# Seven block products instead of eight for six more token tiles, with their operand forms made inside the first MLP pass

## Chip, cores, metric

The kernel runs on one core of a Trainium2 chip. The metric is device time in microseconds (us), the median over runs. TensorE (PE) does the matmuls, with its weight loads shown apart (PEld); VectorE (DVE), ScalarE (ACT) and GpSimd (POOL) do everything elementwise; SyncE (SP) issues nearly all DMAs. PE writes to PSUM (banks 0 to 7 in the kernel), and in the trace each engine runs its instructions in the order in which the program emitted them.

## What is computed

One transformer block on 2048 tokens of width 640, all float32:

```python
xn  = layernorm(x)
qkv = xn @ wqkv                                   # 32 heads of 20
phi = concat(softmax(p), softmax(-p)),  p = q or k @ w_phi   (per head)
o   = phi_q (phi_k^T v) / (phi_q (phi_k^T 1) + 1e-6)          # linear attention
out = x + o @ wo + gelu(layernorm(xn) @ w1 + b1) @ w2 + b2    # 1728 hidden units
```

Each float32 operand is split into a high and a low part, and a product is three matmuls (high·high, high·low, low·high).

## The kernel before, in words

**Layout.** Tokens are cut into four blocks of 512 (b = 0 to 3), each of four tiles of 128 (t = 0 to 15); the 640 features are five slices of 128 (c = 0 to 4). `y[b]` holds the normalised input of block b as a high and a low part.

**Stage 1, first MLP pass (to 212 us).** `Mlp.passes(g, b, ws)` handles two hidden groups of 128 (pass g = 0 to 6) for block b = 0 or 1. Its first half computes the two hidden groups, five three-matmul products each; `gelu` then puts GELU and the rounding to the high part on ACT and the low part on DVE. Its second half, emitted after the first half of the next pass, computes five output columns of two products each into PSUM banks 5, 6 and 7 in turn (`self.po`), and DVE adds each column to `acc[b]` (L338). So the fourth column can't start before DVE has read the first one, and the fifth not before the second. After each second half `take` splits a weight tile: two roundings on ACT (L60), two differences on POOL (L63).

`tick()` is called after every three-matmul product (0.68 us of PE), and advances a generator, `mlp.beside`, that emits other work between the products. In this stage it is `prep()`, whose list `events` holds a tick for each step: it loads slices of x for blocks 2 and 3 (`xs[c, b]`, tile name `xq`), centres them (POOL, L797), scales them (DVE, L800), rounds them (ACT, L804), takes the low part and stores both parts to DRAM (DVE L808 and SP L810). For each pair of slices q = 0, 1 it then combines them in place for the later MLP pass (`combine`, POOL L820). For q = 0 the list starts at `base` = 8, for q = 1 at 52. A tick fixes only the order in which steps join the queues; when they run depends on what they wait for.

For blocks 0 and 1 `turned_forms()` makes differences of the four 128 by 128 blocks of y ("forms"), their high and low parts, and stores them in `f_dram`.

**Stage 2, projections (212 to 426 us).** For each token tile q, k and v are computed against weights held in `wkv_`. An ordinary tile (`plan_part`) takes two parts of 512 columns, one of 320, and one of 512 for v: 15 matmuls each. Tiles 2 to 7 go in pairs instead (`plan_pair`): the two 512-column parts of two tiles and two row slices form 2x2 block products, which take seven products of sums of blocks instead of eight (names a11, s1 to s4 for weights, b11, t1 to t4 for the input); the fifth row slice is added plainly (`rest`). `load_forms(t)` fetches the forms of a pair from `f_dram` into tile `w0`. `plan_sums` makes s1 to s4. The feature maps follow as chains of steps on DVE, POOL and ACT (`plan_features`), and `plan_kv` accumulates phi_k^T v two tiles later. `plan_wo` splits a fifth of the output weights: load, round, subtract, store.

A planner (`Plan`) orders all this: each step has an engine, a cost and the steps it follows, due times are counted back from PE's order, and it emits the queues accordingly. The last eight parts (`TAIL`) belong to tiles 14 and 15.

**Stage 3** is the MLP for blocks 2 and 3 with the attention's second half beside it, then the output product.

Of the kernel before, what the change touches and what calls it, by code (L numbers as in the profile page):

```python
# [8 lines left out]
F32 = mybir.dt.float32  # L9
# [6 lines left out]
P = 128  # L16
# [34 lines left out]
def tile_kernel(ctx: ExitStack, tc: tile.TileContext, x, xT, wkT, wqT, wv, wphi, wo, w1, b1, w2, b2,  # L51
# [43 lines left out]
    f_dram = [tc.dram_tile([2, P, 2, 2, 2, 2 * P], F32, name=f"f{b}") for b in range(2)]  # L95
# [670 lines left out]
    def prep():  # L766
        ahead = []
        more = more_stats()
        for i, job in enumerate(jobs):
            for k, _ in enumerate(prep_fold(job, ahead, None if i else first_done)):  # L770
                if k == 0 and i < 6:
                    ahead = raws(jobs[i + 1])
                if i > 0 and k % 3 == 1:
                    next(more, None)
                yield

        for _ in more:
# [12 lines left out]

        def load(c, b):
            xs[c, b] = gp.tile([P, 512], F32, name="xq", bufs=4)
            with tc.issue_after(loads[1]):
                nc.sync.dma_start(xs[c, b], xT[c * P:(c + 1) * P, b * 512:(b + 1) * 512])

        def centred(c, b):
            nc.gpsimd.tensor_tensor(xs[c, b], xs[c, b], mr[b][:, 0], op=ALU.subtract)  # L797

        def scaled(c, b):
            nc.vector.tensor_tensor(xs[c, b], xs[c, b], mr[b][:, 1], op=ALU.mult)  # L800

        def hi(*at):
            hls[at] = gp.tile([P, 2, 512], F32R, name="t")
            nc.scalar.activation(hls[at][:, 0], xs[at], AF.Copy)  # L804

        def lo(*at):
            hl = hls.pop(at)
            nc.vector.tensor_tensor(hl[:, 1], xs[at], f(hl[:, 0]), op=ALU.subtract)  # L808
# [12 lines left out]

        def combined_lo(q, i):
            at = combined(q, i)[0]
            hl = hls.pop(at)
            nc.vector.tensor_tensor(hl[:, 1], xs[at], f(hl[:, 0]), op=ALU.subtract)
            nc.sync.dma_start(t_dram[q][:, i], f(hl))

        for n, step in enumerate(raw_sums(0, temps)):
            events.append((118 + 3 * n, len(events), step, ()))
        base = 8  # L830
        for q in range(3):
            tiles = [(c, b) for c in range(2 * q, min(2 * q + 2, KC)) for b in range(2, 4)]
            for n, at in enumerate(tiles):
                late = 6 * (at == (KC - 1, 3))
                for after, step in ((-6, load), (0, centred), (3, scaled), (5 + late, hi), (7 + late, lo)):
                    events.append((base + 5 * n + after, len(events), step, at))
            base += 5 * len(tiles) + 5
            if q < 2:
                for n, i in enumerate((0, 2, 1, 3)):
                    for after, step in ((0, combine), (3, lambda q, i: hi(*combined(q, i)[0])), (5, combined_lo)):  # L840
                        events.append((base + 4 * n + after, len(events), step, (q, i)))
                base += 19
        tick = 0
        for at, _, step, args in sorted(events, key=lambda e: e[:2]):
            while tick < at:
                tick += 1
                yield
            step(*args)
# [281 lines left out]
            nc.sync.dma_start(ed[q], ets[b][n][32 * q:32 * q + 32])  # L1130

    fts, ets = {}, {}
    SPLITS = [(8, 1), (8, 3), (9, 1), (9, 3), (10, 1)]
# [5 lines left out]
    def load_y(b):  # L1139

        y[b] = [yp.tile([P, KC, 512], F32R, name=f"y{p}{b % 2}") for p in range(2)]
        for p in range(2):
            nc.sync.dma_start(f(y[b][p]), y_dram[b - 2][p])

    def load_forms(t):
# [196 lines left out]
        if (t, 1 - n) in got:  # L1342
            plan_features(t, "k", j, got[t, 0][0], got[t, 1][0])

    at, got = {}, {}
    yts = {}

    def plan_pair(t):
# [41 lines left out]
        def bank_of(i):  # L1390
            return lambda: held[i]

        z = pe(a, "a11", "b11", True)
# [7 lines left out]
        z = pe(a, "s3", "t3", False, *z12)  # L1401
# [15 lines left out]
        _, q = plan_narrow(t, 0, a)  # L1417
        plan_features(t, "q", 2, d21[1], q)
        plan_wide(t, b1)
        plan_kv(t - 1, c)  # L1420
        _, q = plan_narrow(t + 1, 1, a)
        plan_features(t + 1, "q", 3, d22[1], q)
        plan_wide(t + 1, b1)

    def next_forms(t):
        if t < 6:
            yts[t + 2] = load_forms(t + 2)
        else:
            for q in range(2):
                for p in range(2):  # L1430
                    nc.sync.dma_start(f(wkv_[p][:, 2 * q, 512:1024]), s_dram[:, q, p])

    def plan_sums():

        last = [rp.tile([P, D], F32R, name=f"r{1 + p}")[:, :512] for p in range(2)]
        ways = [mtile(5, F32R), mtile(6, F32R)]
        ways = [third(0), *([w[:, p] for p in range(2)] for w in ways), last]
        ts = wp.tile([P, 4, D], F32, name="w0").rearrange("p i d -> p (i d)")
        ts = [ts[:, i * 512:i * 512 + 512] for i in range(4)]

        def splits(q, ts, ways, after):
            ops = []
# [31 lines left out]
        acc[2] = own["a"].tile([P, KC, 512], F32, name="acc2")  # L1474
        load_acc(2)

    def plan_wo(kc, *after):

        raw = {}

        def load():
            raw["lo"] = rp.tile([P, D], F32, name="r1")
            nc.sync.dma_start(raw["lo"], wo[kc * P:(kc + 1) * P, :])

        def hi():
            raw["hi"] = rp.tile([P, D], F32R, name="r2")
            nc.scalar.activation(raw["hi"], raw["lo"], AF.Copy)

        def lo():
            nc.gpsimd.tensor_tensor(raw["lo"].bitcast(F32R), raw["lo"], f(raw["hi"]), op=ALU.subtract)  # L1490

        def store():
            for w, wd in zip((f(raw["hi"]), raw["lo"]), wo_dram):
                nc.sync.dma_start(wd[:, kc, :], w)

        a = plan.add("SP", 0.7, load, *after)
        b = plan.add("ACT", 0.66, hi, a)
        c = plan.add("POOL", 1.9, lo, b)
        return [plan.add("SP", 1.4, store, c)]

    def first_weights():
        nonlocal mlp
# [35 lines left out]
        plan_part(t, i, n % 3)  # L1538
    for op in thirds:
        op[3] = (*op[3], at[1, 1])  # L1540
    for t in range(2, 8, 2):
        if t == 4:
            plan.add("PE", 0.0, lambda: load_y(2))
        plan_pair(t)
    plan.add("PE", 0.0, lambda: load_y(3))
    n, wo_done = 0, ()
    for t, i in [(t, i) for t in range(8, 14) for i in range(4)] + TAIL:
        plan_part(t, i, n % 3)
        n += 1
        tk = {(15, 1): 13, (15, 3): 14}[t, i] if (t, i) in ((15, 1), (15, 3)) else t - 2 if t < 15 and i == max(1, 10 - t) else None  # L1550
        if tk is not None:
            plan_kv(tk, n % 3)
            n += 1
        if (t, i) == (9, 0):
            plan.add("SP", 3.0, load_acc2, at[t, i])
        if (t, i) in SPLITS:
            wo_done = plan_wo(SPLITS.index((t, i)), at[t, i], *wo_done)
# [621 lines left out]
```

## Time and profile before

| | |
|---|---|
| median of 3 runs | 699.6 us (699.12 to 699.75) |
| the profiled execution | 699.7 us, its span 697.9 us |
| PE busy | 690.7 us (99%) |
| PEld, DVE, POOL, ACT busy | 582.0, 538.3, 493.7, 373.0 us |
| DMA | 117.06 MB, mean 168 GB/s |
| granted TensorE clock | 1.000 |

The span runs from the first to the last instruction. Successive matmuls overlap, so the rows show each at 0.39 us although a 512-column one starts about every 0.227 us. In a timeline row the columns are start, duration (of all merged instructions, with their count as x), engine, line, operation, output and inputs; a bracket gives idle time before it and what ended it.

### The profile page before, as it was taken

How to read it: one execution, taken by the hardware profiler on the slowest of the kernel's cores; microseconds unless marked ns; L12 is line 12 of the kernel's file. 1: busy time of each engine (PE TensorE's matmuls, PEld its weight loads, DVE VectorE, ACT ScalarE, POOL GpSimd, SP SyncE). 2: the span in 40 equal slices, each digit the busy share in tenths (PEclk: the TensorE clock that was granted, in tenths of full speed). 3: DMA queues.
4: the chain of work that ended last, by engine and by line, in shares of the span. 5: the costliest groups of instructions: out<-in, count | busy, mean ns of one | idle time of the engine just before them, and what ended most of it. 6: DMA issues, size and time to landing. Idle time of an engine off the chain costs nothing.

```text
span 697.9 us, 9867 instructions
## 1 busy us (share of the span) xinstructions
PE 690.7 (99%) x3313; PEld 582.0 (83%) x3313; DVE 538.3 (77%) x889; ACT 373.0 (53%) x633; POOL 493.7 (71%) x368
## 2 busy tenths in 40 slices
PE   9999999999999999999999999999999999999998
PEld 7888888888888888888888888888888888888886
DVE  7769564888766989997879778948678687689783
ACT  6435654444443644545554636457676666659350
POOL 3717684756267587889899879648689997677930
PEclk9999999999999999999999999999999999999999
DMA  9816857674622115554723736774355648871222
GB/s 328 261 50 192 245 160 230 222 250 161 203 93 124 61 62 210 137 170 170 170 76 99 178 101 256 225 215 128 110 159 159 180 152 295 283 277 60 77 75 106
DMA packets 72376, 117.06 MB, mean 168 GB/s; under 512 B 8054, under 2 KB 36502, under 8 KB 70318
## 3 DMA queue, kind: packets, MB, share of 16 engines
q1 hardware_dynamic: 69846, 114.32, 51.2%
q10 hardware_dynamic: 2480, 2.11, 1.0%
q8 instruction: 26, 0.43, 0.3%
q14 instruction: 24, 0.20, 0.1%
HBM read 76.62 MB, written 39.79 MB: 167 GB/s over the span
## 4 chain that ended last, share of the span: by engine, by line
PE 95%; DVE 3%; issue 1%; DMA 0%; ACT 0%; DVEq 0%; ACTq 0%
PE bank L996 23%; PE bank L69 19%; PE bank L70 19%; PE bank L71 19%; PE bank L1367 4%; PE bank L1109 2%; PE bank L650 2%; PE bank L1720 1%; PE bank L1721 1%; PE bank L1371 1%; PE bank L556 1%; PE bank L314 1%; PE bank L334 1%; PE bank L315 1%; PE bank L333 1%
## 5 line engine op out<-in xcount | busy, mean ns | idle before, releaser
L69 PE MATMUL bank<-m,w 128*128 128x512 f32 x288 | 112.9, 392 | 0.0
L70 PE MATMUL bank<-m,w 128*128 128x512 f32 x288 | 112.2, 390 | 0.5 <-DVE m L63 0.5
L71 PE MATMUL bank<-m,w 128*128 128x512 f32 x266 | 103.6, 389 | 0.0
L996 PE MATMUL bank<-wkh,y 128*128 128x512 f32 (+1 forms) x360 | 101.0, 355 | 0.0
L69 PE MATMUL bank<-y,w 128*128 128x512 f32 (+1 forms) x256 | 99.6, 389 | 0.4 <-DVE v L1095 0.4
L70 PE MATMUL bank<-y,w 128*128 128x512 f32 (+1 forms) x256 | 98.8, 386 | 0.0
L71 PE MATMUL bank<-y,w 128*128 128x512 f32 (+1 forms) x246 | 95.0, 386 | 0.0
L63 POOL TENSOR_TENSOR w<-r,w 128x640 fp32r<-128x640 f32 x29 | 49.5, 1719 | 34.6 <-ACT w L60 28.1
L996 PEld LDWEIGHTS bank<-wkh,y 128*128 128x128 f32 x360 | 65.0, 188 | 8.1
L70 PEld LDWEIGHTS bank<-m,w 128*128 128x128 f32 x288 | 54.1, 188 | 11.8 <-DVE m L63 0.9
L996 PE MATMUL bank<-wkl,y 128*128 128x512 f32 (+1 forms) x180 | 63.6, 354 | 0.0
L69 PEld LDWEIGHTS bank<-m,w 128*128 128x128 f32 x288 | 54.1, 188 | 11.4 <-issue 0.4
L71 PEld LDWEIGHTS bank<-m,w 128*128 128x128 f32 x266 | 49.9, 188 | 10.4
L338 DVE TENSOR_TENSOR acc<-bank,acc 128x512 f32<-128x512 f32 x70 | 47.2, 683 | 13.6 <-PE bank L71 8.0
L996 PE MATMUL bank<-w,y 128*128 128x512 f32 x240 | 57.5, 391 | 0.0
L69 PEld LDWEIGHTS bank<-y,w 128*128 128x128 f32 x256 | 48.1, 188 | 10.9 <-DVE v L1095 0.5
L1036 DVE TENSOR_REDUCE sm<-m 128x64 f32<-128x1280 f32 x32 | 47.1, 1471 | 11.8 <-ACT m L1031 11.8
L70 PEld LDWEIGHTS bank<-y,w 128*128 128x128 f32 x256 | 48.1, 188 | 9.4
L1028 POOL TENSOR_TENSOR m<-m,mx 128x640 f32<-128x640 f32 x32 | 45.9, 1434 | 12.2 <-DVE w L1061 5.7
L71 PEld LDWEIGHTS bank<-y,w 128*128 128x128 f32 x246 | 46.2, 188 | 9.4
L1031 ACT ACTIVATE m<-m,rs_all 128x1280 f32<-128x1280 f32 x32 | 43.7, 1366 | 16.4 <-POOL m L1028 16.4
L1714 POOL TENSOR_TENSOR e<-e,m 128x512 fp32r<-128x512 f32 x28 | 41.7, 1491 | 15.1 <-ACT m L1713 15.0
(291 smaller groups left out, 1684.3 us busy)
## 6 DMA issues: line engine op xcount, KB each, us to landing
r<-in_w SPq DMA_DIRECT2D x52, 320.0 KB
e<-e SPq DMA_DIRECT2D x40, 256.0 KB
e<-acc SPq DMA_DIRECT2D x52, 160.0 KB
t<-t SPq DMA_DIRECT2D x8, 512.0 KB
acc<-in_xT SPq DMA_DIRECT2D x3, 1280.0 KB
w<-f SPq DMA_DIRECT2D x3, 1024.0 KB
tf<-t SPq DMA_DIRECT2D x2, 1536.0 KB
xb<-in_x SPq DMA_DIRECT2D x8, 320.0 KB
```

Of the source, the lines that this page charges most:

```text
L63: eng.tensor_tensor(lo, src, f(hi), op=ALU.subtract)
L69: nc.tensor.matmul(ps, lh, rh, start=first, stop=False, **kw)
L70: nc.tensor.matmul(ps, lh, rl, start=False, stop=False, **kw)
L71: nc.tensor.matmul(ps, ll, rh, start=False, stop=last, **kw)
L338: nc.vector.tensor_tensor(acc[b][:, m, :], pw, acc[b][:, m, :], op=ALU.add)
L650: nc.tensor.matmul(ps[:, u * nh * DF:(u + 1) * nh * DF], raw[:nh * DH, u * P:(u + 1) * P], wpt[:nh * DH, g, :nh, 1:], start=True, stop=True)
L996: nc.tensor.matmul(ps, lh[:, kc, c], rh[:, kc], start=n == 0, stop=n == 3 * KC - 1)
L1028: subs[n, t] = nc.gpsimd.tensor_tensor(ep[:, :, s], a, b, op=ALU.subtract)
L1031: exps[n, t] = nc.scalar.activation(e, e, AF.Exp, scale=rs_all[:, t:t + 1])
L1036: nc.vector.tensor_reduce(sm, e.rearrange("p a (h f) -> p (a h) f", f=DH), axis=AX, op=ALU.add)
L1367: nc.tensor.matmul(ps, left(yn, pl, q), right(w, pr, q), start=first and q == 0 and n == 0, stop=False, skip_group_check=True)
L1714: mlp.after(1, lambda: nc.gpsimd.tensor_tensor(pl, e, f(ph), op=ALU.subtract))
```

## The change

Tiles 8 to 13 also go through `plan_pair`. Their forms are made in `prep()`: for q = 0 and q = 1, four differences on POOL, two roundings on ACT and two low parts with two stores each, 512 columns wide for block 2 (tiles 8 to 11) and 256 wide for block 3 (tiles 12 and 13). The forms lie in the tiles `acc2` and `s12` until they are stored. `w0` becomes one standing place for the fetched forms, so `plan_sums` takes its temporary places elsewhere. The output weights are split in ten halves, two beside each pair from tile 4 on, instead of five fifths beside tiles 8 to 10. The loads of the next stage's first weights move from tile 11 to tile 14.

```diff
-    f_dram = [... name=f"f{b}") for b in range(2)]
+    f_dram = [... name=f"f{b}") for b in range(NB)]
...
+        def form_sub(b, q, i):
+            w = 512 if b == 2 else 2 * P
+            r0, r1 = (xs[c, b][:, :w].rearrange("p (i j n) -> p i j n", j=2, n=P) for c in (2 * q, 2 * q + 1))
+            z0, z1 = (z.rearrange("p (i j n) -> p i j n", j=2, n=P) for z in form_places[b][:2])
+            out, x0, x1 = ((z0[:, :, 0], r0[:, :, 1], r0[:, :, 0]), (z0[:, :, 1], r1[:, :, 1], r0[:, :, 1]),
+                           (z1[:, :, 1], r1[:, :, 1], z0[:, :, 0]), (z1[:, :, 0], r1[:, :, 0], z1[:, :, 1]))[i]
+            nc.gpsimd.tensor_tensor(out, x0, x1, op=ALU.subtract)
+
+        def form_hi(b, q, i):
+            z = form_places[b]
+            nc.scalar.activation(z[2 + i].bitcast(F32R), z[i], AF.Copy)
+
+        def form_lo(b, q, i):
+            z = form_places[b]
+            nc.vector.tensor_tensor(z[i].bitcast(F32R), z[i], z[2 + i], op=ALU.subtract)
+            n = z[i].shape[1] // (2 * P)
+            for p, part in enumerate((z[2 + i], z[i])):
+                nc.sync.dma_start(f_dram[b][:n, :, q, i, p]..., part...)
+
+        own["t"] = own["s"].tile([P, 512], F32, name="s12")
+        form_places = {2: temps[:4], 3: [z[:, o:o + 2 * P] for z in (spare[0], own["t"]) for o in (0, 2 * P)]}
...
+            if q < 2:
+                for b, at, his, los in ((2, 14, (16, 18), (18, 20)), (3, 19, (21, 23), (23, 25))):
+                    for i in range(4):
+                        events.append((base + at + i, len(events), form_sub, (b, q, i)))
+                    for i in range(2):
+                        events.append((base + his[i], len(events), form_hi, (b, q, i)))
+                        events.append((base + los[i], len(events), form_lo, (b, q, i)))
...
 def load_forms(t):
-        place = wp.tile([P, 4, D], F32R, name="w0").rearrange("p i d -> p (i d)")[:, :16 * P]
+        place = forms_place[0][:, :16 * P]
...
 def plan_pair(t):
+        for n in range(t - 4, t - 2) if t > 2 else ():
+            plan_wo(n, at[t, 0])
...
 def next_forms(t):
-        if t < 6:
+        if t < 12:
...
 def plan_wo(n, *after):          # was (kc, *after), 640 columns at once
+        kc, cols = n // 2, slice(n % 2 * 320, n % 2 * 320 + 320)
...
-    for t in range(2, 8, 2):
+    for t in range(2, 14, 2):
...
-    for t, i in [(t, i) for t in range(8, 14) for i in range(4)] + TAIL:
+    for t, i in TAIL:
...
-        if (t, i) == (11, 0):
-            fetched = plan.add("SP", 1.4, first_weights, at[t, i], *wo_done)
-        if (t, i) == (12, 3):
+            fetched = plan.add("SP", 1.4, first_weights, at[t, i])      # at (14, 0)
             w1_done = plan_pair_splits(at[t, i], fetched)
```

More of the change, by code (lines that the diff above doesn't have):

```diff
@@ L94, in tile_kernel @@
     a_dram = [tc.dram_tile([P, KC, 512], F32, name=f"a{b}") for b in range(2)]
-    f_dram = [tc.dram_tile([2, P, 2, 2, 2, 2 * P], F32, name=f"f{b}") for b in range(2)]
+    f_dram = [tc.dram_tile([2, P, 2, 2, 2, 2 * P], F32, name=f"f{b}") for b in range(NB)]
     s_dram = tc.dram_tile([P, 2, 2, 512], F32, name="s21")
@@ L826, in combined_lo @@
             nc.sync.dma_start(t_dram[q][:, i], f(hl))
+        def form_sub(b, q, i):
[13 more added lines that the diff above has]
+            for p, part in enumerate((z[2 + i], z[i])):
+                nc.sync.dma_start(f_dram[b][:n, :, q, i, p].rearrange("k p n -> p k n"), part.rearrange("p (k n) -> p k n", k=n))
+        own["t"] = own["s"].tile([P, 512], F32, name="s12")
+        form_places = {2: temps[:4], 3: [z[:, o:o + 2 * P] for z in (spare[0], own["t"]) for o in (0, 2 * P)]}
         for n, step in enumerate(raw_sums(0, temps)):
@@ L1433, in plan_sums @@
     def plan_sums():
-        last = [rp.tile([P, D], F32R, name=f"r{1 + p}")[:, :512] for p in range(2)]
+        forms_place.append(wp.tile([P, 4, D], F32R, name="w0").rearrange("p i d -> p (i d)"))
+        last = [forms_place[0][:, 16 * P:], rp.tile([P, D], F32R, name="r1")[:, :512]]
         ways = [mtile(5, F32R), mtile(6, F32R)]
         ways = [third(0), *([w[:, p] for p in range(2)] for w in ways), last]
-        ts = wp.tile([P, 4, D], F32, name="w0").rearrange("p i d -> p (i d)")
-        ts = [ts[:, i * 512:i * 512 + 512] for i in range(4)]
+        et = turns[4].rearrange("p c n -> p (c n)")
+        ts = [et[:, :512], et[:, 512:1024], rp.tile([P, D], F32, name="r2")[:, :512], mtile(0)[:, 0, :512]]
         def splits(q, ts, ways, after):
@@ L1475, in load_acc2, with plan_wo @@
         load_acc(2)
-    def plan_wo(kc, *after):
+    def plan_wo(n, *after):
+        kc, cols = n // 2, slice(n % 2 * 320, n % 2 * 320 + 320)
         raw = {}
         def load():
-            raw["lo"] = rp.tile([P, D], F32, name="r1")
-            nc.sync.dma_start(raw["lo"], wo[kc * P:(kc + 1) * P, :])
+            r = rp.tile([P, D], F32, name="r2")
+            raw.update(lo=r[:, :320], hi=r[:, 320:])
+            nc.sync.dma_start(raw["lo"], wo[kc * P:(kc + 1) * P, cols])
         def hi():
-            raw["hi"] = rp.tile([P, D], F32R, name="r2")
-            nc.scalar.activation(raw["hi"], raw["lo"], AF.Copy)
+            nc.scalar.activation(raw["hi"].bitcast(F32R), raw["lo"], AF.Copy)
         def lo():
-            nc.gpsimd.tensor_tensor(raw["lo"].bitcast(F32R), raw["lo"], f(raw["hi"]), op=ALU.subtract)
+            nc.gpsimd.tensor_tensor(raw["lo"].bitcast(F32R), raw["lo"], raw["hi"], op=ALU.subtract)
         def store():
[L1493 to L1499, printed above, removed]
+            for w, wd in zip((raw["hi"], raw["lo"]), wo_dram):
+                nc.sync.dma_start(wd[:, kc, cols], w)
+        a = plan.add("SP", 0.7, load, *after, *wo_done)
+        b = plan.add("ACT", 0.4, hi, a)
+        c = plan.add("POOL", 1.0, lo, b)
+        wo_done[:] = [plan.add("SP", 1.4, store, c)]
     def first_weights():
@@ L1540, in tile_kernel @@
         op[3] = (*op[3], at[1, 1])
-    for t in range(2, 8, 2):
-        if t == 4:
-            plan.add("PE", 0.0, lambda: load_y(2))
+    for t in range(2, 14, 2):
+        if t in (4, 8):
+            plan.add("PE", 0.0, lambda t=t: load_y(2 + t // 8))
         plan_pair(t)
-    plan.add("PE", 0.0, lambda: load_y(3))
-    n, wo_done = 0, ()
-    for t, i in [(t, i) for t in range(8, 14) for i in range(4)] + TAIL:
+    n = 2
+    for t, i in TAIL:
         plan_part(t, i, n % 3)
         n += 1
-        tk = {(15, 1): 13, (15, 3): 14}[t, i] if (t, i) in ((15, 1), (15, 3)) else t - 2 if t < 15 and i == max(1, 10 - t) else None
-        if tk is not None:
-            plan_kv(tk, n % 3)
+        if (t, i) in ((14, 1), (15, 1), (15, 3)):
+            plan_kv({(14, 1): 12, (15, 1): 13, (15, 3): 14}[t, i], n % 3)
             n += 1
-        if (t, i) == (9, 0):
+        if (t, i) == (14, 0):
             plan.add("SP", 3.0, load_acc2, at[t, i])
-        if (t, i) in SPLITS:
-            wo_done = plan_wo(SPLITS.index((t, i)), at[t, i], *wo_done)
-        if (t, i) == (11, 0):
-            fetched = plan.add("SP", 1.4, first_weights, at[t, i], *wo_done)
-        if (t, i) == (12, 3):
+            fetched = plan.add("SP", 1.4, first_weights, at[t, i])
             w1_done = plan_pair_splits(at[t, i], fetched)
```

10 lines of the change are left out of this document (5 added, 5 removed).

## The prediction

> **What bounds the kernel.** I read the page's busy times and chain first, then PE by stage, then the queues in the two places where the change puts work. PE is busy for 690.7 of the 697.9 us, and the chain that ends last is PE for 95%.
>
> ```profile
> span 697.9 us, 9867 instructions
> PE 690.7 (99%) x3313; PEld 582.0 (83%) x3313; DVE 538.3 (77%) x889; ACT 373.0 (53%) x633; POOL 493.7 (71%) x368
> PE 95%; DVE 3%; issue 1%; DMA 0%; ACT 0%; DVEq 0%; ACTq 0%
> ```
>
> So a matmul removed is time removed, and a wait that reaches PE is time added: PE has no idle stretch in which to hide it. The table by stage (length, then busy time of PE, PEld, DVE, ACT, POOL, clock, DMA share, GB/s) has the third pair in its first row and two ordinary tiles in its second; the two rows below it, of the sums over v of tiles two apart, show that two ordinary tiles take 376.94 - 349.57 = 27.37 us.
>
> ```profile
> 289.34:315.39 26.05, 26.05 (x138) 22.66 (x136) 24.33 (x40) 12.86 (x21) 20.74 (x16) 1.00 0.64 180
> 342.76:370.13 27.37, 27.37 (x143) 23.80 (x142) 22.32 (x35) 15.68 (x23) 24.83 (x18) 1.00 0.41 118
> 349.57 1.29 PE L1109 MATMUL bank<-w,v 128*128 128x240 f32 x10
> 376.94 1.29 PE L1109 MATMUL bank<-w,v 128*128 128x240 f32 x10
> ```
>
> **The gain.** A pair needs 7 x 6 + 4 x 3 = 54 wide matmuls where two tiles need 60, and takes 26.05 us instead of 27.37: 1.32 us less, 0.22 for each matmul. Three more pairs: **-4.0 us**.
>
> **The forms, first place (q = 0).** They are 16 differences, 8 roundings and 8 low parts, of kinds that the tile xq shows (min/median/max in ns).
>
> ```profile
> L804 ACT ACTIVATE t<-xq x18: 618/633/636, 123.1 to 191.4; 128x512 fp32r<-128x512 f32 x18
> L890 POOL TENSOR_TENSOR xq<-xq x16: 728/738/752, 54.2 to 105.6; 128x256 f32<-128x256 f32 x16
> L797 POOL TENSOR_TENSOR xq<-xq,m x10: 1285/1296/1751, 120.9 to 181.7; 128x512 f32<-128x512 f32 x10
> L800 DVE TENSOR_TENSOR xq<-xq,m x10: 676/1258/2046, 122.2 to 187.2; 128x512 f32<-128x512 f32 x10
> L808 DVE TENSOR_TENSOR t<-xq,t x10: 674/888/1290, 124.4 to 193.5; 128x512 fp32r<-128x512 f32 x10
> ```
>
> A difference for block 2 has L890's shape: 0.74 us. Their busy time matters less than their places in the queues. For q = 0 the differences for block 2 have ticks 22 to 25, their roundings 24 and 26, their low parts 26 and 28; for block 3 the differences 27 to 30, roundings 29 and 31, low parts 31 and 33. What stands there already is read from the rows below (POOL, ACT, DVE and PE, each in order of time): the centring of tick 23 (132.53), the scaling of 26 (134.30), the rounding of 28 (136.09). The two GELUs of a pass come five ticks apart. The first's low part follows the scaling of 26 directly (135.99), the second's runs at 137.97, and three column sums two ticks apart fit between it and the low part of tick 38 (140.37). So the GELUs are at ticks 26 and 31, the sums at 33, 35 and 37.
>
> ```profile
> 132.53 1.74 POOL L797 TENSOR_TENSOR xq<-xq,m 128x512 f32<-128x512 f32 x1
> ...
> 136.09 0.63 ACT L804 ACTIVATE t<-xq 128x512 fp32r<-128x512 f32 x1 [2.68 <-DVE xq L800]
> 136.63 0.64 ACT L293 ACTIVATE bank<-bank,b1t 128x512 f32<-128x512 f32 x1
> 137.31 0.60 ACT L60 ACTIVATE m<-bank 128x512 fp32r<-128x512 f32 x1
> 137.81 0.63 ACT L804 ACTIVATE t<-xq 128x512 fp32r<-128x512 f32 x1
> ...
> 134.30 1.76 DVE L800 TENSOR_TENSOR xq<-xq,m 128x512 f32<-128x512 f32 x1 [1.18 <-POOL xq L797]
> 135.99 0.68 DVE L63 TENSOR_TENSOR m<-bank,m 128x512 fp32r<-128x512 f32 x1
> 137.97 0.68 DVE L63 TENSOR_TENSOR m<-bank,m 128x512 fp32r<-128x512 f32 x1
> 138.57 1.87 DVE L338 TENSOR_TENSOR acc<-bank,acc 128x512 f32<-128x512 f32 x3
> 140.37 0.68 DVE L825 TENSOR_TENSOR t<-xq,t 128x512 fp32r<-128x512 f32 x1
> ...
> 139.40 0.41 PE L69 MATMUL bank<-m,w 128*128 128x512 f32 x1
> ```
>
> This is one chain already: centring, scaling, rounding, GELU, its low part, column sum. The first of the three sums ends at about 138.57 + 0.69 = 139.26, and PE starts the fourth column, into the same bank, at 139.40. The slack is 0.14 us.
>
> The new steps stand inside this chain. POOL comes to them at 132.53; four differences and the centring at its shortest end at 132.53 + 4 x 0.74 + 1.29 = 136.78. ACT waits for the last of them with the second rounding (tick 26), and the first GELU, whose product is long done, is queued behind it: rounding 0.54 (136.09 to 136.63), GELU and its rounding 1.18 (136.63 to 137.81), the rounding of 28 0.54, two of half width 0.64, and 1.34 from the start of the second GELU to its low part on DVE (136.63 to 137.97): 141.02. With 0.60 for that and 0.35 (half of 0.68) for the form's low part of tick 33 the first sum starts at 141.97 instead of 138.57, 3.40 later, and PE loses 3.40 - 0.14 = **3.3 us at least**.
>
> At most: the scaling took 1.76 us beside POOL's work where such an operation takes 0.68 at its shortest, and the centring 1.74. If the centring costs 0.46 more and each of four low parts on the path (ticks 28, 30, 31, 33) waits 0.6, it is 3.3 + 0.5 + 2.4 = 6.2. The median scaling lies 0.58 above the shortest, the median L808 0.21, so something like half of them wait: I take two, **4.5 us**. The Trainium skill ("SBUF — State Buffer", section "SBUF: two separate sides") makes it an exclusive lock: a DVE operation with two SBUF inputs and a GpSimd operation block each other for a whole instruction. By that rule all four would wait, and the place would cost about 5.7; with shared bandwidth only, near 3.3.
>
> **Second place (q = 1).** Everything is 44 ticks later: differences 66 to 69 around a centring of 67, the second rounding 70 before the GELU of 71, low parts 70, 72, 75, 77 around the sums of 73, 75, 77.
>
> ```profile
> 158.19 2.99 POOL L797 TENSOR_TENSOR xq<-xq,m 128x512 f32<-128x512 f32 x2
> ...
> 162.74 0.66 ACT L293 ACTIVATE bank<-bank,b1t 128x512 f32<-128x512 f32 x1 [0.35 <-PE bank L71]
> ...
> 159.95 1.77 DVE L800 TENSOR_TENSOR xq<-xq,m 128x512 f32<-128x512 f32 x1 [1.18 <-POOL xq L797]
> 164.68 0.68 DVE L338 TENSOR_TENSOR acc<-bank,acc 128x512 f32<-128x512 f32 x1
> ...
> 166.62 0.39 PE L69 MATMUL bank<-m,w 128*128 128x512 f32 x1
> ```
>
> The first sum ends at 165.36 and the fourth column starts at 166.62: slack 1.26. The first centring is over when the scaling starts, 159.95; a difference, a centring and three differences end at 159.95 + 0.74 + 1.29 + 2.22 = 164.20. Rounding 0.54, GELU to low part 1.34, that low part 0.60, the form's of tick 72 0.61: the sum starts at 167.29, 2.61 late, and 1.35 reach PE. Before the second sum stand two more low parts (0.61 and 0.35), so the fifth column waits 0.2 again: 1.55 at least. With the centring slow and three waits of 0.6, 3.8. With two waits, **2.7 us**.
>
> **What I cost at nothing.** *Stores*: 16 DMAs, 3.1 MB. On SP they wait for the low parts, and the loads of weights and of xq queue behind them; but weights issued at 145.04 are first read at 153.59, and the DMA engines are half free around the first place. If that cover fails, a late weight stops PE; I leave 0.5 for it.
>
> ```profile
> 135.00:145.00 10.00, 10.00 (x46) 8.18 (x45) 9.20 (x12) 4.94 (x8) 5.62 (x5) 1.00 0.47 153
> 145.04 0.38 SPq L251 DMA_DIRECT2D r<-in_w  x1
> 153.59 1.35 ACT L60 ACTIVATE w<-r 128x640 fp32r<-128x640 f32 x2
> 412.70 1.57 POOL L1517 TENSOR_TENSOR w<-r,w 128x640 fp32r<-128x640 f32 x1
> 426.68 0.50 PE L69 MATMUL bank<-y,w 128*128 128x512 f32 x1 [0.39 <-DVE v L1095]
> ```
>
> *Output weights*: two halves a pair, 1.6 us of POOL (a tile of 640 columns, L1517, takes 1.57), covered by the 5.3 us that POOL is idle in a pair. *Form loads*: three more of 1 MB, each fetched a pair ahead, as for tiles 4 and 6 now. *Tail*: the last difference of the first MLP weights ends at 414.27, 12 us before their stage starts at 426.68; a load some us later is covered, and past that it would stop PE.
>
> **Sum.** -4.0 + 4.5 + 2.7 = +3.2. The profiled execution took 699.7, so 702.9; the median shown is 0.1 lower: **702.8 us**. With both places at their least, -4.0 + 4.8 = +0.8 (700.4); at their most, -4.0 + 10.0 + 0.5 = +6.5 (706.1).
>
> **Rivals.** *The forms are hidden* (not slower). POOL is idle for 4.4 of 10 us around the first place, and its steps run ahead of PE where their data is there; if the differences do, the GELUs are not held and only the gain is left: 695.6. It decides if the first sums still end by 139.40 and 166.62. Against it stands the chain above, with 0.14 us to spare. Chance 0.18. *The stalls about equal the gain*, 2.6 to 5.4 in all: within 0.2% of before (1.4 us, about what a measurement of this kernel can tell from no change), 699.6; 0.12. *DVE becomes the bound of the pairs*: 24.33 of 26.05 now, with more POOL work beside it. Against: PE has no wait in the pair shown, and the next ones add only halves of output weights. If each stretched to 27.37 the gain would be lost beside the stalls: 706.8; 0.06. *The clock falls in a stall*: the first matmuls of the run, after idle time, took 6.75 us for 18, which at 0.22 take 4.0.
>
> ```profile
> 1.31 6.75 PE L584 MATMUL bank<-m 128*128 128x512 f32 x18 [1.31 <-POOL m L582]
> ```
>
> That is 2.8 us lost; once, after the longer stall, it gives 705.6; 0.08. The Trainium skill ("TensorE: Matmul & The Clock Gate", section "What's actually happening") puts PE at half clock after an idle window of about 3.4 us; the granted clock reads 1.00 in every row here, so none shows it.
>
> **Chances.** The forecast, stalls above the gain, has 0.56 and its own range 701.0 to 706.1. Faster 0.18, same 0.12, slower 0.56 + 0.06 + 0.08 = 0.70. The range for 8 in 10, 695.8 to 706.2, leaves out about half of the first rival and the upper parts of the last two.
>
> **What would show it.** PE idle before the first matmul of a column, ended by DVE's column sum, near 139 and near 171; a GELU on ACT behind a rounding that waits for POOL; six pairs of 26.05 us; projections starting some 7 us later. I am wrong if these waits are missing, if pairs 8 to 12 are longer, or if PE waits elsewhere.

## The result and the profile after

The changed kernel takes 718.9 us (median of 5 runs, 717.2 to 720.9); the kernel before, run beside it, 699.1. The ratio is 1.0276, with a 95% interval of 1.0262 to 1.0290. The forecast was 702.8: the direction was right, the size was not, and the time lies outside the range.

The page of the changed kernel, its first lines and its chain:

```profile
span 716.6 us, 9974 instructions
PE 691.6 (97%) x3295; PEld 580.7 (81%) x3295; DVE 549.6 (77%) x915; ACT 376.8 (53%) x646; POOL 506.5 (71%) x389
PE 77%; DVE 6%; POOL 6%; DMA 5%; issue 3%; ACT 2%; SPq 0%; POOLq 0%; DVEq 0%; ACTq 0%
```

PE has 18 matmuls less and yet is busy 0.9 us more, and the chain that was 95% PE is now 77% PE, with DVE, POOL, DMA and ACT in it. In the costliest groups (busy, mean ns, then idle time before and what ended it), PE's idle time stands in two places in the program:

```profile
L69 PE MATMUL bank<-m,w 128*128 128x512 f32 x288 | 114.0, 396 | 9.7 <-DVE acc L338 9.7
L1025 PE MATMUL bank<-w,y 128*128 128x512 f32 x240 | 59.6, 401 | 8.1 <-DVE v L1124 8.1
```

The first is the column of the first MLP pass that the prediction spoke of. The second, almost as much, is in the projections behind the pairs, where it expected nothing.

**The pairs do what they should.** The table by stage has a pair in its row, and the sums over v of two pairs in a row stand 26.14 us apart:

```profile
313.00:339.15 26.15, 26.15 (x138) 22.74 (x137) 23.09 (x40) 13.75 (x23) 22.48 (x17) 1.00 0.46 166
337.80 1.29 PE L1138 MATMUL bank<-w,v 128*128 128x240 f32 x10
363.94 1.29 PE L1138 MATMUL bank<-w,v 128*128 128x240 f32 x10
```

PE never waits in it. Three times 27.37 - 26.15 is 3.7 us gained.

**The first place.** POOL, ACT, DVE and PE in order of time:

```profile
132.62 1.19 POOL L834 TENSOR_TENSOR acc<-xq 128x256 f32<-128x256 f32 x1
133.78 1.27 POOL L797 TENSOR_TENSOR xq<-xq,m 128x512 f32<-128x512 f32 x1
135.02 0.73 POOL L834 TENSOR_TENSOR acc<-xq 128x256 f32<-128x256 f32 x1
135.71 2.51 POOL L834 TENSOR_TENSOR acc<-xq,acc 128x256 f32<-128x256 f32 x2
...
139.97 2.95 POOL L820 TENSOR_TENSOR xq<-xq 128x512 f32<-128x512 f32 x2
...
138.25 0.63 ACT L838 ACTIVATE acc<-acc 128x512 fp32r<-128x512 f32 x1 [1.84 <-POOL acc L834]
138.79 0.64 ACT L293 ACTIVATE bank<-bank,b1t 128x512 f32<-128x512 f32 x1
...
141.09 0.65 ACT L293 ACTIVATE bank<-bank,b1t 128x512 f32<-128x512 f32 x1
...
140.70 1.09 DVE L842 TENSOR_TENSOR acc<-acc 128x512 fp32r<-128x512 f32 x1
141.72 1.75 DVE L808 TENSOR_TENSOR t<-xq,t 128x512 fp32r<-128x512 f32 x1
...
143.73 0.68 DVE L63 TENSOR_TENSOR m<-bank,m 128x512 fp32r<-128x512 f32 x1
144.33 0.88 DVE L842 TENSOR_TENSOR acc<-acc,s 128x256 fp32r<-128x256 f32 x1
145.13 1.88 DVE L338 TENSOR_TENSOR acc<-bank,acc 128x512 f32<-128x512 f32 x3
...
145.86 0.79 PE L69 MATMUL bank<-m,w 128*128 128x512 f32 x1 [6.25 <-DVE acc L338]
```

It is the chain of the prediction, link by link: the second rounding (L838) waits for the last difference, the GELU (L293) is queued behind it, DVE's column sums (L338) behind the low parts, and PE behind the first sum.

**The last two waits.** A half's load, ACT and PE at 404; then POOL, a half's load, ACT, DVE and PE at 438:

```profile
395.69 0.34 SPq L1518 DMA_DIRECT2D r<-in_wo  x1
402.26 0.47 ACT L1521 ACTIVATE r<-r 128x320 fp32r<-128x320 f32 x1 [5.73 <-DMA r<-in_wo]
404.51 0.70 PE L1025 MATMUL bank<-w,y 128*128 128x512 f32 x2 [1.75 <-DVE v L1124]
...
432.42 1.53 POOL L1551 TENSOR_TENSOR w<-r,w 128x640 fp32r<-128x640 f32 x1
433.98 0.35 SPq L1518 DMA_DIRECT2D r<-in_wo  x1
437.10 0.47 ACT L1521 ACTIVATE r<-r 128x320 fp32r<-128x320 f32 x1 [10.56 <-issue]
437.48 0.36 ACT L1119 ACTIVATE v<-bank,rs_all 128x132 fp32r<-128x132 f32 x1
438.10 0.36 DVE L1124 SCALAR_TENSOR_TENSOR v<-bank,rs_all,v 128x132 fp32r<-128x132 f32 x1 [9.22 <-ACT m L1037]
438.51 5.57 PE L1025 MATMUL bank<-w,y 128*128 128x512 f32 x15 [6.33 <-DVE v L1124]
```

ACT comes in order to the rounding of a half of the output weights (L1521) whose load has not landed. Behind the rounding, 0.38 us later, stands the reading of a PSUM bank (L1119), then DVE's step on it (L1124), and PE needs the bank. The rounding is worth 0.47 us of ACT; its place in the queue is worth 6.33 us of PE. The two loads are late for different reasons. The one at 395.69 is issued about 2 us behind the load of the third accumulator (1280 KB, at 393.60) and its rounding starts 6.57 us later. The one at 433.98 waits to be issued: its raw tile (`r2`) is still held by the next stage's weights until POOL has taken their low part (L1551, to 433.95). The bracket of the rounding there says "issue", but the profile's list of who waited for L1551 has this rounding, with 10.6 us.

**The clock.** In the table by stage the column behind the busy times is the granted clock:

```profile
146.00:150.00 4.00, 4.00 (x12) 3.17 (x13) 2.29 (x4) 0.60 (x2) 0.00 (x0) 0.63 0.46 171
172.00:178.00 6.00, 2.87 (x14) 2.06 (x12) 3.10 (x5) 3.54 (x7) 5.76 (x8) 1.00 0.69 238
178.00:182.00 4.00, 3.64 (x15) 2.70 (x16) 3.79 (x7) 1.05 (x2) 0.64 (x2) 1.00 0.69 236
438.50:442.50 4.00, 3.99 (x9) 3.14 (x10) 4.00 (x7) 3.19 (x6) 1.58 (x2) 0.50 1.05 410
```

After the waits of 6.25 and 6.33 us PE works on, but at 0.63 and 0.50 of its clock: 4.00 x 0.37 + 4.00 x 0.50 = 3.5 us more. After the second place's wait of 3.13 us (second and third row) it did not fall in this execution.

**The account**, profile to profile (716.6 - 697.9 = +18.7): the pairs -3.7; waits of PE +17.8 (6.25, then 3.13 + 0.36, then 1.75 + 6.33 + 0.34, less the 0.39 that the kernel before had at the end of its projections); the clock +3.5. That makes +17.6; 1.1 us stays unassigned. It lies in PE's busy time, since PE's idle time grew by 17.8 in all (25.0 against 7.2). Matmul rows of 0.39 us that start every 0.227 us overlap, so a start that is late by up to 0.16 us leaves no gap; that the 1.1 us is made of such delays is not shown.

### The profile page after: what moved, and what is told of

It is laid out like the page before. It is cut to its first block, busy times and chain, and to the rows that moved or that the text cites. A ratio compares the mean times of both kernels' runs of the same rounds, so it can differ in the third digit from the quotient of the medians.

```text
span 716.6 us, 9974 instructions
## 1 busy us (share of the span) xinstructions
PE 691.6 (97%) x3295; PEld 580.7 (81%) x3295; DVE 549.6 (77%) x915; ACT 376.8 (53%) x646; POOL 506.5 (71%) x389
## 4 chain that ended last, share of the span: by engine, by line
PE 77%; DVE 6%; POOL 6%; DMA 5%; issue 3%; ACT 2%; SPq 0%; POOLq 0%; DVEq 0%; ACTq 0%
PE bank L69 16%; PE bank L71 16%; PE bank L70 16%; PE bank L1025 11%; PE bank L1397 7%; DMA xq<-in_xT 2%; PE bank L1401 2%; PE bank L650 2%; PE bank L1138 2%; POOL m L1057 1%; PE bank L1748 1%; PE bank L1749 1%; POOL acc L834 1%; POOL xq L797 1%; DMA r<-in_wo 1%
## 5 line engine op out<-in xcount | busy, mean ns | idle before, releaser
L1025 PE MATMUL bank<-w,y 128*128 128x512 f32 x240 | 59.6, 401 | 8.1 <-DVE v L1124 8.1
L1025 PE MATMUL bank<-wkh,y 128*128 128x320 f32 (+1 forms) x240 | 63.1, 337 | 0.0
L1025 PEld LDWEIGHTS bank<-w,y 128*128 128x128 f32 x240 | 45.7, 193 | 17.7 <-DVE v L1124 6.6
L338 DVE TENSOR_TENSOR acc<-bank,acc 128x512 f32<-128x512 f32 x70 | 47.2, 683 | 13.9 <-PE bank L71 8.3
L1078 POOL TENSOR_TENSOR m<-m,w 128x1280 f32<-128x1280 f32 x16 | 43.4, 2712 | 18.6 <-DVE w L1071 14.7
L1057 POOL TENSOR_TENSOR m<-m,mx 128x640 f32<-128x640 f32 x32 | 40.9, 1279 | 15.0 <-DVE mx L1047 7.0
```

Source lines behind the costliest of these rows:

```text
L338: nc.vector.tensor_tensor(acc[b][:, m, :], pw, acc[b][:, m, :], op=ALU.add)
L1025: nc.tensor.matmul(ps, lh[:, kc, c], rh[:, kc], start=n == 0, stop=n == 3 * KC - 1)
L1057: subs[n, t] = nc.gpsimd.tensor_tensor(ep[:, :, s], a, b, op=ALU.subtract)
L1078: nc.gpsimd.tensor_tensor(e3, e3, w.unsqueeze(2).to_broadcast([P, 2 * H, DH]), op=ALU.mult)
```

## The experiments

The theory that the traces gave: two independent causes, each a burst of small steps standing in an in-order queue ahead of something that PE needs (the forms on POOL, ACT and DVE in the first pass; the rounding of a late half on ACT in the projections), and a clock that falls behind each long wait. The rivals: the forms' differences alone hold DVE; the late waits come from somewhere else than the halves; the clock falls for a reason other than the wait. Line numbers shift by some lines from kernel to kernel.

**e1_forms_only**: the kernel before with the form steps at the changed kernel's places, and nothing that reads them.

```diff
 (before)
+            if q < 2:
+                for b, at, his, los in ((2, 14, (16, 18), (18, 20)), (3, 19, (21, 23), (23, 25))):
+                    ...form_sub, form_hi, form_lo
```

> The kernel before, with the new differences, roundings, low parts and stores for tiles 8 to 13 added at the changed kernel's ticks, but nothing reads them: tiles 8 to 13 stay ordinary. Queue theory (the new steps hold GELUs and column sums in two places of the first pass): PE waits of 6.3 and 3.5 us as in the changed kernel, about 1.5 us at a lower clock after the first, and nothing else: 699.1 + 11.3 = 710.4 us. Rival (these waits need the rest of the change, through memory or DMA): at most the 7.2 us that the prediction worked out, 699 to 706.

712.8 us against 699.9, ratio 1.0173 [1.0154, 1.0192]. The waits come back without a single pair, and both are followed by half clock:

```profile
146.00 0.80 PE L69 MATMUL bank<-m,w 128*128 128x512 f32 x1 [6.40 <-DVE acc L338]
179.32 0.80 PE L69 MATMUL bank<-m,w 128*128 128x512 f32 x1 [3.48 <-DVE acc L338]
146.00:151.00 5.00, 5.00 (x12) 3.94 (x13) 2.44 (x4) 1.15 (x3) 0.00 (x0) 0.50 0.52 153
179.30:186.00 6.70, 6.68 (x17) 5.25 (x18) 4.76 (x8) 1.88 (x3) 2.12 (x3) 0.57 0.55 184
```

The forms alone cost 12.9 us by the medians. The profiled execution took 715.3, which is 15.4 more than 699.9: 9.9 of waits and 5.00 x 0.50 + 6.68 x 0.43 = 5.4 of clock. Here the wait of 3.48 us had its fall, where 3.13 had none.

**e2_forms_late**: the changed kernel with roundings and low parts some 15 ticks later.

```diff
-    ((2, 14, (16, 18), (18, 20)), (3, 19, (21, 23), (23, 25)))
+    ((2, 14, (34, 35), (36, 37)), (3, 19, (36, 37), (38, 39)))
```

> The changed kernel, with roundings and low parts of the forms 15 to 18 ticks later (behind the column sums of the pass), the differences where they were. Queue theory: the GELUs are no longer behind a rounding that waits for POOL, so the waits of 6.3 and 3.5 us shrink to 0 to 2 each, with perhaps 1 to 3 us new behind later column sums, and the clock does not fall there: 718.9 - 7 = 709 to 714 us. Rival (the amount of added work on POOL and DVE makes the waits, wherever it stands): the same sum of waits, 717 to 720.

719.2 us, ratio 1.0273 [1.0257, 1.0288]: no gain, a miss, and the rival's number. The two old waits were gone, but the steps found new things to stand in front of:

```profile
155.85 0.50 PE L69 MATMUL bank<-m,w 128*128 128x512 f32 x1 [2.34 <-DVE acc L338]
196.82 0.49 PE L314 MATMUL bank<-y,w 128*128 128x512 f32 x1 [3.29 <-DVE w L63]
```

with the clock at 0.59 behind each. PE's waits in the pass sum to 7.5 us instead of 9.7, and one more fall of the clock took the difference. Later in the same queues is no cure by itself. That the work would cost this wherever it stands is settled by e5 below, which has as much of it.

**e3_halves_early**: the changed kernel with the halves issued one pair earlier (beside tiles 2 to 11 instead of 4 to 13).

```diff
-        for n in range(t - 4, t - 2) if t > 2 else ():
+        for n in range(t - 2, t) if t < 12 else ():
```

> The changed kernel, with the ten halves of the output weights one pair earlier (tiles 2 to 11 instead of 4 to 13). Theory of the shared raw tile (the last half's load stands behind the first MLP weights in tile r2, and ACT's rounding of it holds the evacuations of the projections): the waits of 1.75 and 6.3 us and the slow matmuls after the longer one (2.0) go: 718.9 - 10 = 709 us. Rival (the pairs leave a backlog on DVE and POOL, which comes due in the last tiles): the wait of 6.3 keeps most of its size, 715 to 719.

712.3 us, ratio 1.0174 [1.0159, 1.0189]: 6.6 us less, expected about 10. The 6.33 us wait and its slow matmuls are gone, and in the stretch from 420 to 445 PE is busy for 24.80 of 25.00 us at full clock. The wait near 405 stayed, at 1.73.

**e4_pe_fill**: the changed kernel with 18 unread matmuls into a spare bank ahead of the column that waits, so that PE waits less while the others do the same.

```diff
+                if (g, b, m) == (3, 1, 3):
+                    idle = banks.tile([P, 512], F32, name="bank3")
+                    for _ in range(18):
+                        nc.tensor.matmul(idle, ws[0][2][:, 0:P], hid[0][0], start=True, stop=True)
```

> The changed kernel, with 18 matmuls into an unused PSUM bank put before the fourth column of the first place, where PE now waits 6.25 us; their result is read by nobody. Clock theory (PE runs slow after a long idle stretch): the idle stretch is about 2 us and the seven matmuls after it start every 0.23 us instead of 0.43, 1.4 us less, 717.5 us. Rival (the first matmuls after any wait are slow, by what they read or write): they stay at 0.43, 718.9 us.

718.8 us (one run), the rival's number. The wait shrank to 2.37 us, and the clock fell all the same, not in the wait but after it:

```profile
145.83 0.50 PE L69 MATMUL bank<-m,w 128*128 128x512 f32 x1 [2.37 <-DVE acc L342]
139.00:146.00 7.00, 4.63 (x21) 3.54 (x20) 5.98 (x8) 4.15 (x9) 5.05 (x5) 1.00 0.63 218
146.00:150.00 4.00, 4.00 (x11) 3.12 (x12) 2.26 (x4) 0.73 (x2) 0.00 (x0) 0.57 0.47 171
```

So the expected gain did not come: either a wait of 2.37 us is long enough for the fall, or the theory is wrong. e8 decides.

**e5_forms_spread**: differences into places of their own; roundings and low parts, six of each and 512 columns wide, after the second combination.

```diff
-    for b, at, his, los in ((2, 14, (16, 18), (18, 20)), (3, 19, (21, 23), (23, 25))):
-        ...
+    for b, ats in ((2, (8, 22, 23, 24)), (3, (24, 25, 26, 27))):
+        ...                            # form_sub alone
+    for at, one in zip((97, 104, 108, 116, 120, 124), ((2, 0, 0), (2, 0, 1), (2, 1, 0), (2, 1, 1), (3, 0, 0), (3, 1, 0))):
+        events.append((at, len(events), form_hi, one))
+        events.append((at + 2, len(events), form_lo, one))
```

> Only the first pass is changed: the differences stay near their old places (spread a little), but write into places of their own, and the roundings and low parts, six of each of 512 columns, wait until the second combination is over, where DVE and POOL have more idle time. Theory (the burst of differences, roundings and low parts together is what holds DVE at the two places, and its half-clock matmuls come with it): both places' waits (6.25 and 3.49 us) shrink to under 1 us each and no matmuls run at half clock there, so about 719 - 9 - 3 = 707 us. Rival (the differences alone, through GpSimd's hold on VectorE, are the bulk): half or more of the 9.7 us of waits stays, 712 to 716. Second rival (the late steps find a new place to hold DVE or ACT, as in the run with the forms put off by 15 ticks): 710 to 714, with a PE wait past 185 us.

708.7 us, ratio 1.0120 [1.0105, 1.0135]: 10.2 us less than the changed kernel, and the first theory's number within 1.7. PE is busy throughout the first place at full clock, and so it is from 175 to 185; a new wait of 0.84 us came near 195.

```profile
140.00:150.00 10.00, 10.00 (x45) 8.28 (x45) 6.11 (x8) 5.07 (x9) 9.84 (x8) 1.00 0.58 188
```

**e6_halves_free**: e3 (the halves one pair earlier; its expectation says two) with the loads of the third accumulator and of the first MLP weights planned behind the halves' last store.

```diff
-            plan.add("SP", 3.0, load_acc2, at[t, i])
-            fetched = plan.add("SP", 1.4, first_weights, at[t, i])
+            plan.add("SP", 3.0, load_acc2, at[t, i], *wo_done)
+            fetched = plan.add("SP", 1.4, first_weights, at[t, i], *wo_done)
```

> The first pass is as in the changed kernel; the ten halves are issued two pairs earlier, and the load of the third accumulator and of the first MLP weights wait until the halves are stored. Theory (ScalarE waits in order for a half's late load, once behind the accumulator's load and once behind the weights): the 1.73 us near 405 goes, and the 6.33 us near 438 stays away with its slow matmuls, so about 1.7 us under the earlier halves alone (712.3): 710.5 us. Rival (the 1.7 us near 405 has another cause than the transfer before it): 712.3. Second rival (the put-off loads are now late for the MLP's first block): a new PE wait after 440 us, 713 or more.

712.0 us, ratio 1.0162 [1.0141, 1.0184], the first rival's number; the wait stayed, at 1.65. But the edit did not do what it says. On SP's queue the weights' load (L363) and the accumulator's (L520) still went out ahead of the half's (L1518), so the plan's order is not what orders this queue:

```profile
393.86 0.33 SPq L363 DMA_DIRECT2D r<-in_w  x1
...
395.33 0.38 SPq L520 DMA_DIRECT2D acc<-in_xT  x1
397.33 0.34 SPq L1518 DMA_DIRECT2D r<-in_wo  x1
```

It tells nothing against the theory; e9 repeats it with the order tied on the queue itself.

**e7_both**: e5 and e6 together.

> Both of these edits in one kernel. Theory (the four waits and their half-clock matmuls are all that the pairs' gain of 4.1 us was lost to, and they add): 719 - 12 - 8.5 = 698.5, and by the account from the other side 699.4 - 4.1 + about 1 us of small waits = 696.3; so 696 to 699, faster than the kernel before. Rival (a load that is off the waits now, such as the sixteen stores' traffic or the later roundings, costs as much): 700 to 706.

700.6 us, ratio 1.0008 [0.9998, 1.0018]: not to be told from no change, 2 us over what was expected and at the lower end of the rival's range. As shares of the kernel before, e5 took off 1.56 points of the changed kernel's 2.76, e6 1.14, and both 2.68: the two causes add. What was left in the trace were waits of 0.86 us near 195 and 1.47 us near 394.

**e8_fill26**: e4 with 26 matmuls.

```diff
-                    for _ in range(18):
+                    for _ in range(26):
```

> The changed kernel with 26 matmuls more, into a bank that nothing reads, ahead of the column that waits at the first place, so that PE's own wait there should be about 6.25 - 26 x 0.215 = 0.7 us; the end of the wait, set by DVE, stays. Theory (the half clock follows a PE wait of some length): no half-clock matmuls from 146 to 150 us, PE's busy time less its 5.6 us of fill some 1.5 to 2 us below the changed kernel's. Rival (the half clock follows the disturbance of DVE, or the time, and not PE's wait): the matmuls there start 0.43 us apart as before.

718.0 us (one run). PE's wait at the first place is gone, and with it the fall: the same stretches as in e4 now read 1.00. The second place, with no fill, waits 2.89 us and falls:

```profile
139.00:146.00 7.00, 6.92 (x31) 5.40 (x30) 6.70 (x9) 3.70 (x8) 4.45 (x4) 1.00 0.65 224
146.00:150.00 4.00, 4.00 (x19) 3.32 (x18) 3.33 (x5) 1.41 (x3) 1.65 (x2) 1.00 0.52 157
175.50:182.00 6.50, 6.46 (x16) 5.12 (x17) 4.55 (x8) 1.88 (x3) 1.91 (x2) 0.54 0.50 157
```

So it is PE's own wait that the fall follows, as far as one execution of each shows: DVE was held in this kernel as in e4 (its low parts took 1.12, 1.78 and 0.91 us, there 1.11, 1.78 and 0.88). The whole time hardly moved: the other falls stayed, and that of the second place, where the changed kernel had none, came on top.

**e9_both_queued**: e7 with those two loads tied behind the last half's load on the queue, and the low parts moved a little. In the last two lines each pair is the tick of a rounding and of its low part.

```diff
+            wo_load[:] = [nc.sync.dma_start(raw["lo"], ...).ins]
...
+        with tc.issue_after(wo_load[0]):
             load_acc(2)                    # and mlp.fetch_pair(0, False)
...
-    (97, 99), (104, 106), (108, 110), (116, 118), (120, 122), (124, 126)
+    (97, 99), (104, 110), (114, 117), (117, 120), (121, 124), (125, 128)
```

> The kernel with both edits, with two more: the loads of the third accumulator and of the first MLP weights are tied behind the last half's load on SP's queue (the run before showed them issued at 383.12 and 381.64, ahead of that load at 385.07, though the plan had them later), and the late roundings and low parts are moved a few steps so that no low part stands in front of DVE's accumulations while it waits for ScalarE. Theory (the last 1.47 us wait of the projections is the last half's load behind 1.3 MB of accumulator; the 0.86 us near 195 is the low part at 192.86): both go, 700.6 - 1.5 - 0.9 = 698.2. Rival (the wait of the projections is ScalarE's own order of work and no transfer): it stays at about 1.5, 699.7. Second rival (the accumulator or the weights now come late for the MLP): a wait past 425 us, 700 or more.

698.4 us against 699.4, ratio 0.9995 [0.9983, 1.0007]. The half's load now goes first, lands in time, and ACT waits 0.80 us for it, where the changed kernel waits 5.73 and e7 5.46 at this step; PE's wait near 394 is gone, which settles what e6 left open.

```profile
384.72 0.33 SPq L1525 DMA_DIRECT2D r<-in_wo  x1
385.15 0.38 SPq L363 DMA_DIRECT2D r<-in_w  x1
385.58 0.42 SPq L520 DMA_DIRECT2D acc<-in_xT  x1
387.04 0.47 ACT L1528 ACTIVATE r<-r 128x320 fp32r<-128x320 f32 x1 [0.80 <-DMA r<-in_wo]
```

The low parts, now among the raw sums, made a wait of 1.56 us at 206.03, with no fall behind it.

**e10_diffs_only**: e1 without the roundings, low parts and stores.

> The kernel before with the sixteen differences alone, at the same steps as in the changed kernel and into the same places; the roundings, the low parts and the sixteen stores are left out, so nothing reads the differences. Theory (the roundings and low parts are the bulk of the first pass's loss): PE's two waits are under 1 us each, none followed by half-clock matmuls, 700 to 701.5. Rival (the differences alone hold DVE through GpSimd): waits of 3 us and more at one of the two places at least, 704 to 712.

700.6 us, ratio 1.0015 [1.0006, 1.0025], with PE busy for all of both places (7.00 of 7.00 us from 139, 10.00 of 10.00 from 171). The sixteen differences alone cost about 1 us; the roundings, low parts and stores that stand on them, the other 12.

**e11_one_per_column**: e9 with the low parts two ticks or more apart, all ahead of the raw sums, three of them in place.

```diff
-    (97, 99), (104, 110), (114, 117), (117, 120), (121, 124), (125, 128)
+    (95, 97), (98, 100), (99, 105), (102, 107), (106, 109), (107, 111)
```

> As the queued kernel, but the six late low parts stand two steps or more apart, all ahead of the raw sums, so that one fits between two accumulations of a column (DVE was idle 0.67 us before each of them near 192 to 196); three of the six round into places of the raw tiles and keep their low parts in place, so that the two staging tiles do not hold them up. Theory (the 1.56 us wait at 206.03 was the low parts among the raw sums): it goes and no other wait of over 0.5 us comes, 698.4 - 1.5 = 697.0, some 2.4 us below the kernel before. Rival (DVE has no room anywhere from 184 to 206 us): another wait of 1 to 2 us there, 698 to 699.5.

700.6 us, ratio 1.0011 [1.0000, 1.0021], a miss. The wait at 206 went, but the first rounding waits 3.40 us for its staging tile, and at 188.94 PE waits 1.86 us for a weight's low part on DVE, with the clock at 0.66 behind it:

```profile
183.62 0.63 ACT L848 ACTIVATE t<-acc 128x512 fp32r<-128x512 f32 x1 [3.40 <-DMA t<-t]
188.94 0.50 PE L314 MATMUL bank<-y,w 128*128 128x512 f32 x1 [1.86 <-DVE w L63]
189.00:194.00 5.00, 4.95 (x14) 3.68 (x15) 4.05 (x8) 2.69 (x5) 0.00 (x0) 0.66 0.60 209
```

**e12_later_start**: e11 with two of the six moved.

```diff
-    (95, 97), (98, 100), ...
+    (97, 99), (115, 118), ...
```

> As the run before, with two of its six low parts moved: the first two roundings stood at 183.62 and 184.84 us there, waited for a staging tile's store, and the accumulation behind them let PE wait 1.86 us at 188.94, with half-clock matmuls after it; the first now comes two steps later and the second after the column accumulations, before the raw sums write over its place. Theory (DVE has room for one low part a column from 195 us on, and none before): no PE wait over 0.5 us in the first pass, 700.6 - 1.9 - 1.3 = 697.4, about 2 us below the kernel before. Rival (the small delays that the late steps add up to need no wait of this size): 698.5 to 700.

698.4 us against 699.8, ratio 0.9975 [0.9965, 0.9986]: a quarter of a per cent faster than the kernel before, 1 us over the number expected. Past two waits at 83 and 92 us (0.68 and 0.60) that the kernel before has too, no wait of PE above 0.22 us is left in the first pass, and none above 0.48 behind it:

```profile
span 695.4 us, 9970 instructions
PE 688.1 (99%) x3295; PEld 579.0 (83%) x3295; DVE 547.3 (79%) x913; ACT 377.3 (54%) x644; POOL 506.1 (73%) x389
```

Its projections start at 213.63 where those of the kernel before start at 212.41, and its second MLP at 424.33 instead of 426.68: 3.6 us gained over the pairs, as counted, and 1.2 lost in the first pass. Of these 1.2, 1.0 stands in PE's busy time (210.56 us of that stage against 209.59), not in waits. Where exactly was not followed further.

## Why the prediction was wrong, step by step

The sum was -4.0 + 4.5 + 2.7 = +3.2. Measured by the same terms: -3.7 + 6.25 + 3.49, then two terms that were costed at nothing or left to a rival: +8.0 for the late halves and +3.5 for the clock.

- *The gain*: right. The new pairs take 26.15 us, 0.1 more than the pair in the row.
- *First place*: the mechanism was right, the size was not. Measured 6.25, just past the upper bound of 6.2. Two terms were mis-sized. The larger is the four differences, put at 0.74 each, with nothing above that even in the upper bound, which stretches the centring instead. They ended at 138.22 instead of 136.78: the centring took its shortest (1.27), but three of the differences did not (1.19, and 2.51 for the last two; one took 0.73); that is 1.4. The other is the low parts on DVE, put at 1.2 above the least (two waits of 0.6) and measured at 1.75. The second GELU's low part started at 143.73, 1.3 later than the GELU (141.09 + 1.34) called for, behind a low part of 1.09 and one of 1.75 where such a step takes 0.68; and 0.45 more came from the next, 0.88. The sum started 3.2 us after the least estimate. The Trainium skill ("SBUF — State Buffer", section "SBUF: two separate sides") holds that such DVE and GpSimd operations block each other for a whole instruction. The low part of 1.75 us agrees with it: it ends at 143.47, 0.55 after POOL's second combination (142.92), and takes 0.68 at its shortest. By that rule the prediction put the place at 5.7, the nearer number, in part by luck: the 5.7 has four waits of DVE and none of POOL. No run isolates what slowed the differences; in e10, without the form's low part that DVE starts at 136.93 in the changed kernel, the last of them took 0.74 instead of 1.24.
- *Second place*: the same mechanism, 3.49 against 2.7, below the bound of 3.8; its parts were not taken one by one.
- *Stores and form loads at nothing*: in the changed kernel no wait of PE above 0.25 us ends with a late weight or a form; e5 has all the traffic and runs 10 us faster. Of the 12 us between e10 and e1 the stores' own share was not measured apart.
- *Output weights, "covered by the 5.3 us that POOL is idle in a pair"*: this is the step that failed most. I priced a half by its busy time on POOL and looked for room there. It has a link on ACT as well, and that link waits for a transfer. The halves and the next stage's weights share a raw tile, and the change no longer makes the weights wait for the last half's store. So the weights took the tile first, the last half's load went out at 433.98 only, and the rounding held ACT for 10.56 us and PE for 6.33. e3 took that away (-6.6 us). e9 took away what is left in e7 of the 1.75, a half's load behind that of the accumulator.
- *Tail, "a load some us later is covered"*: it looked at the moved load alone and not at what the move let past. The weights' load was in time; the half behind it was not. The load of the third accumulator moved as well, from tile 9 to tile 14; neither the description of the change nor the prediction names it, and it is the one that the half of the 1.75 stands behind.
- *The clock, a rival with 0.08 and 2.8 us*: it belonged in the sum, under the stalls. e8 shows the fall to follow PE's wait, so a forecast of a wait of 4.5 us had to carry one. The price of 2.8 us was fair: the falls in these traces cost 1.4 to 3.1. That is the second failed step.
- *The forms are hidden* (0.18): false as written, though it can be made true. In e5 and e12 they nearly are, with the roundings elsewhere.
- *DVE bounds the pairs*: false; PE is busy for all of a pair.

## What to carry to other kernels

A step costs what stands behind it in its queue, for as long as its latest input is late; its busy time only says whether it would fit. So for each step that is added or moved, follow every engine that it passes, ask when its input lands, and name what is queued next; where a dependence is dropped, ask which transfer may now go first. And where PE is the bound, a wait can cost more than itself: here 18 of the 19 waits of 1.86 us and more brought a fall of the clock that cost another 1.4 to 3.1 us.

## What the hardware showed that was not expected

*Half clock after short waits.* Behind the start of the program, the traces hold 19 waits of PE of 1.86 us and more (1.86, 2.34, 2.37, 2.88 and so on up to 6.49). All but one came with about 3 to 6 us of half clock once PE was back; the exception is the 3.13 in the changed kernel. Waits of 1.47 to 1.75 us, in nine kernels, had none. After the waits of 2.34, 2.37 and 3.29 us the clock fell only when PE was back at work, 0.6 to 0.7 us after its return, and after the 1.86 (e11) 1.7 us after it. What decides between 3.13 without a fall and 2.88 with one stays open. The Trainium skill ("TensorE: Matmul & The Clock Gate", section "What's actually happening") names an idle window of about 3.4 us; here less was enough, and the measured waits are what to go by on this kernel.
